# Loading one weight matrix in two transfers of unequal height: 16 partitions, then 112

## The chip, the cores and the metric

The kernel runs on one core of a Trainium2 chip. The metric is the device time of one execution in microseconds, the median of several runs. A core has five instruction streams that matter here: TensorE (PE, with its weight loads shown apart as PEld), VectorE (DVE), ScalarE (ACT), GpSimd (POOL) and SyncE (SP). SyncE computes nothing; it issues the transfers between the chip's main memory (HBM) and the on-chip memory (SBUF, 128 partitions), and those are carried out by 16 DMA engines.

## What is computed

One decode step of a transformer block whose attention and feed-forward halves work side by side on the same normalised input, for 4 sequences and one new token each:

```python
xn = layernorm(x)                                   # x: 4 x 1 x 512
q  = (xn @ wq)                                      # wq: 512 x 4096, 32 heads of 128
p  = softmax(q . k_cache * 128**-0.5)               # k_cache: 4 x 32 x 8192 x 128
o  = (p . v_cache) @ wo                             # v_cache like k_cache; wo: 4096 x 512
f  = (silu(xn @ w_gate) * (xn @ w_up)) @ w_down     # 512 x 1792, 1792 x 512
out = x + o + f
```

All arrays are bfloat16. The two caches are 268 MB each, so nearly all of the bytes that have to be read are keys and values; each is used once.

## The kernel before

SBUF holds three large buffers, `slot[0]` to `slot[2]`, each of 128 partitions by 64 KB. A key tile or a value tile is 8 MB, fills one slot, and covers four heads of one sequence; there are 32 of each. The slots are used in turn: while one tile is being worked on, the next two are on their way. All loads are issued by SyncE, in the order in which the code states them, and a load into a slot waits until the work that reads the slot's old content is done.

A tile of keys is turned in place by VectorE (`turn_k`, line 261), multiplied with the queries by TensorE (`score`, line 268), and the softmax weights of it follow (`max_1`, `max_2`, `pt_turn`). The tile of values that belongs to it is then multiplied with these weights (`pv`, line 310) and the result is scaled (`fin`). `begin` and `finish` hold these pieces; a hardware loop (line 408) walks over the 32 tiles.

The change touches what comes ahead of that loop. `wq_t` is `slot[2]`. The matrix wq (4 MB) goes into the first 32 KB of each partition of that slot, one row of 32 KB per partition, by a single transfer of 128 partitions (line 101). The input x (4 rows) goes into the same slot beside it, by two small transfers (lines 102 and 103). The first key tile goes to `slot[0]` (`load_k(0, 0)`, line 95). These four transfers are issued at once, with nothing to wait for.

When x has landed, VectorE normalises it (lines 156 to 172), TensorE turns it (line 177) and multiplies it with wq (lines 183 to 187), and VectorE and ScalarE bring the queries into their place, `qtn` (lines 193 to 200). `build_q` (line 255) spreads the queries of one tile into `zq`, which the scores need. The three feed-forward matrices are loaded into `slot[2]` as soon as wq has been read (`load_ffn`, lines 219 to 221), then comes the second key tile into `slot[1]`. The first key tile is turned and scored, its slot takes the first values (line 98), and the feed-forward half is computed. Then the loop starts.

After the loop's last round the matrix wo is loaded into a slot in 11 pieces (lines 381 and 385), multiplied piece by piece with the attention output (`wo_mm`), and the sum is stored (lines 449 to 451).

Of the kernel before, what the change touches and what calls it, by code (L numbers as in the profile page):

```python
# [15 lines left out]
def kernel(  # L16
# [13 lines left out]
    nc = tc.nc  # L30
    P = nc.NUM_PARTITIONS

    B, Sq, D = A_x.shape
    _, H, Sk, Dh = A_k_cache.shape
# [3 lines left out]
    EC = D // P  # L38
# [43 lines left out]
    wq_t = slot[2]  # L82
    free = [EC * H * Dh]

    def beside_wq(parts, w, dtype=dt.bfloat16):

        n = w * (2 if dtype == dt.float32 else 1)
        c0 = free[0]
        free[0] += n
        assert free[0] <= SLOT  # L90
        ap = wq_t[0:parts, c0:c0 + n]
        return ap.bitcast(dt.float32) if dtype == dt.float32 else ap
# [4 lines left out]
    def load_v(n, s):  # L97
        nc.sync.dma_start(out=slot[s][:], in_=v_all[bass.ds(n, 1), :, :].rearrange("o p f -> (o p) f"))

    x_sb = beside_wq(B, D)  # L100
    nc.sync.dma_start(out=wq_t[:, 0:EC * H * Dh], in_=A_wq.rearrange("(p c) n -> p (c n)", c=EC))
    nc.sync.dma_start(out=x_sb[0:B - 1, :], in_=x_flat[0:B - 1, :])
    nc.sync.dma_start(out=x_sb[B - 1:B, :].rearrange("b (k e) -> b k e", k=2),
                      in_=x_flat[B - 1:B, :].rearrange("b (k e) -> b k e", k=2))
# [86 lines left out]
    for half in range(NH):  # L191
        for r in range(2):
            nc.vector.transpose(out=qt[:, half, :, r, :],
                                in_=q_ps[half][:].rearrange("p (x i r) -> p x i r", x=8, r=2)[:, :, :, r])
# [285 lines left out]
```

## Time and profile before

| | |
|---|---|
| time, median of 3 runs | 1279.57 us (1279.52 to 1279.66) |
| span of the profiled run | 1278.0 us |
| bytes moved by DMA | 550.90 MB |
| TensorE busy | 694.6 us, 54% |
| VectorE busy | 790.5 us, 62% |
| mean clock granted to TensorE | 0.778 of full speed |

A reader should know four views. The page gives the busy time of each engine, and the span in 40 slices with the share of time that the DMA engines were busy. Its list of DMA issues gives, for each load, how many there were, how large, and the median time from issue to landing; a load that stands in a queue behind others shows a long time there although its own bytes take less. The timeline shows instructions in order of time, with the idle time before each and what ended it. The chain of waits follows the work that ended last back to what released it, step by step.

### The profile page before, as it was taken

To read this page: it belongs to the slowest core of one execution; us is meant where nothing else is said; L and a number is where in the kernel's file an instruction comes from. 1 tells how busy PE (TensorE), PEld (TensorE's weight loads), DVE (VectorE), ACT (ScalarE), POOL (GpSimd) and SP (SyncE) were. 2 spreads that over 40 slices of the span, in tenths; PEclk is the share of its full clock that TensorE was granted. 3 is DMA by queue.
4 is the path that set the end of the run, shared out by engine and by line. 5 is a ranking of instruction groups with operands and counts; after the bars stand their busy time and mean duration, and the time that the engine had idled before them with its cause. 6 is when DMAs were issued, how large, how long until landed. Compare 5 with 4: busy or idle time off the path is not lost.

```text
span 1278.0 us, 11913 instructions
## 1 busy us (share of the span) xinstructions
PE 694.6 (54%) x4507; PEld 306.5 (24%) x4507; DVE 790.5 (62%) x743; ACT 28.8 (2%) x70; POOL 13.1 (1%) x12
## 2 busy tenths in 40 slices
PE   1765455665445665445664446664446654456655
PEld 0322122222212222122222212221222222122222
DVE  5777655666655766655757555766556666556662
ACT  1000000000000000000000000000000000000000
POOL 3000000000000000000000000000000000000000
PEclk9977668877778877678877778876778777688868
DMA  9999999999999999999999999999999999999998
GB/s 401 446 435 429 432 434 441 427 437 431 443 429 429 439 435 437 427 439 433 441 427 437 431 441 431 429 437 437 437 427 439 433 441 427 437 431 441 431 424 346
DMA packets 11689, 550.90 MB, mean 431 GB/s; under 512 B 1304, under 2 KB 1824, under 8 KB 2720
## 3 DMA queue, kind: packets, MB, share of 16 engines
q1 hardware_dynamic: 11680, 550.78, 99.6%
q8 instruction: 6, 0.10, 0.0%
q14 instruction: 3, 0.02, 0.0%
HBM read 550.77 MB, written 0.00 MB: 431 GB/s over the span
## 4 chain that ended last, share of the span: by engine, by line
PE 49%; DVE 22%; another core or an unknown queue 14%; DMA 9%; issue 5%; DVEq 0%; SPq 0%; ACT 0%; PEld 0%; PEldq 0%
PE sps L73 36%; DVE slot L261 12%; PE oacc L73 9%; DMA slot<-in_A_k_cache_dram 7%; DVE ptz L291 4%; DVE zq L255 2%; PE xps L73 2%; DVE oacc L323 2%; DVE o L324 2%; PE mps L73 1%; DMA slot<-in_A_wo_dram 1%; DMA slot<-in_A_x_dram 1%; PE mps L277 1%; DVE rcp L300 0%
## 5 line engine op out<-in xcount | busy, mean ns | idle before, releaser
L73 PE MATMUL sps<-slot,zq 128*128 128x512 bf16 x2048 | 518.2, 417 | 392.2 <-DVE slot L261 392.2
L261 DVE STREAM_TRANSPOSE slot<-slot 128x2048 uint32<-128x2048 uint32 (+1 forms) x194 | 561.5, 2958 | 207.5 <-DMA slot<-in_A_k_cache_dram 207.4
L73 PEld LDWEIGHTS <-zq 128*128 128x128 bf16 x2048 | 211.4, 104 | 686.8 <-issue 343.5
L291 DVE STREAM_TRANSPOSE ptz<-p__117 32x512 bf16<-32x512 bf16 x128 | 89.9, 703 | 86.9 <-PE mps L73 83.9
L73 PE MATMUL oacc<-slot,ptz 128*16 128x512 bf16 x2112 | 130.8, 390 | 7.0 <-issue 3.9
L73 PE MATMUL xps<-rowy,o 128*128 128x4 f32 x66 | 18.3, 348 | 157.6 <-DVE o L324 157.6
L272 DVE TENSOR_REDUCE mx<-sps 128x1 f32<-128x512 f32 x32 | 22.1, 692 | 100.9 <-PE L73 69.3
L73 PEld LDWEIGHTS <-ptz 128*16 128x16 bf16 x2112 | 58.7, 111 | 64.8 <-issue 24.7
L73 PEld LDWEIGHTS xps<-rowy,o 128*128 128x128 f32 x66 | 16.0, 302 | 160.0 <-issue 110.3
L285 ACT ACTIVATE p__117<-sps,nb 128x512 bf16<-128x512 f32 x32 | 22.0, 687 | 1169.9 <-PE oacc L73 758.9
L255 DVE COPY zq<-qtn 32x4 bf16 (+1 forms) x128 | 29.9, 233 | 3.5
L323 DVE TENSOR_TENSOR oacc<-oacc,rowu 128x512 f32<-128x512 f32 x33 | 23.1, 699 | 7.7 <-PE L73 6.7
L324 DVE TENSOR_REDUCE o<-oacc 128x128 f32<-128x512 f32 x33 | 22.8, 691 | 1.1
L280 DVE TENSOR_REDUCE nm<-mps 128x4 f32<-128x64 f32 x32 | 7.2, 224 | 23.4 <-PE L73 23.4
L319 DVE TENSOR_TENSOR otn_nat<-xps,rcp 128x4 f32 (+1 forms) x33 | 5.3, 162 | 23.6 <-PE xps L73 22.2
L73 PEld LDWEIGHTS mps<-rowb,rs 128*128 128x128 f32 x64 | 9.5, 186 | 13.2 <-issue 13.2
L73 PE MATMUL mps<-rowb,rs 128*128 128x4 f32 x64 | 12.3, 263 | 0.0
L277 PE MATMUL mps<-ident_f,mx 128*128 128x128 f32 x32 | 10.5, 328 | 0.0
L373 POOL MEMSET slot<- 128x11264 bf16 x1 | 9.5, 9484 | 18.9 <-DVE qtn L200 18.9
L277 PEld LDWEIGHTS mps<-ident_f,mx 128*128 128x128 f32 x32 | 4.3, 134 | 13.6 <-DVE mx L272 12.4
L73 PE MATMUL yo_ps<-slot,ident 4*4 4x256 bf16 x2 | 0.4, 368 | 13.2 <-DMA slot<-in_A_x_dram 13.2
L300 DVE RECIPROCAL rcp<-mps 128x4 f32<-128x4 f32 x32 | 5.8, 182 | 1.0
(60 smaller groups left out, 64.6 us busy)
## 6 DMA issues: line engine op xcount, KB each, us to landing
slot<-in_A_wq_dram SPq DMA_DIRECT2D x1, 4096.0 KB, 12.3
slot<-in_A_v_cache_dram SPq DMA_DIRECT2D x1, 4096.0 KB, 44.5
slot<-in_A_v_cache_dram SPq DMA_DIRECT2D x2, 2048.0 KB, 50.6
slot<-in_A_wo_dram SPq DMA_DIRECT2D x7, 512.0 KB, 18.2
slot<-in_B_w_gate_dram SPq DMA_DIRECT2D x1, 1792.0 KB, 16.6
slot<-in_B_w_up_dram SPq DMA_DIRECT2D x1, 1792.0 KB, 19.6
slot<-in_B_w_down_dram SPq DMA_DIRECT2D x1, 1792.0 KB, 22.5
slot<-in_A_k_cache_dram SPq DMA_DIRECT2D x32, 51.5
```

The lines of the kernel that those rows point to most:

```text
L73: nc.tensor.matmul(out_ap, lhsT=lhsT, rhs=rhs, start=start, stop=True, skip_group_check=True, **kw)
L255: nc.vector.tensor_copy(out=zq[q0:q1, :, XO + a * QB], in_=qtn[q0:q1, bass.ds(n * 4, 4)])
L261: nc.vector.transpose(out=ap, in_=ap)
L272: nc.vector.reduce_max(out=mx[:], in_=sps[:], axis=AX.X)
L277: nc.tensor.matmul(mps[:, 0:P], lhsT=mx[:, 0:1].to_broadcast([P, P]), rhs=ident_f[:, :], is_transpose=True, start=True, stop=True, skip_gr ...
L280: nc.vector.tensor_reduce(out=nm[:], in_=by_row(mps[:, 0:P]), axis=AX.X, op=ALU.max, negate=True)
L285: nc.scalar.activation(out=p_[:], in_=sps[:], func=ACT.Exp, bias=nb[:, 0:1], scale=qscale, accum_out=rs[:])
L291: nc.vector.transpose(out=ptz[y * QB:(y + 1) * QB, :, y, :, :].rearrange("p s u x -> p s (u x)"), in_=p_[y * QB:(y + 1) * QB, :].rearrange ...
L300: nc.vector.reciprocal(out=rcp[c % NSLOT][:], in_=mps[:, P:P + HT])
L323: nc.vector.tensor_tensor(out=o_, in0=o_, in1=rowu[:].unsqueeze(2).to_broadcast([P, NV, Dh]), op=ALU.mult)
L324: nc.vector.reduce_sum(out=o1[:], in_=o_.rearrange("p u d -> p d u"), axis=AX.X)
L373: nc.gpsimd.memset(slot[2][:, w3:SLOT], 0.0)
```

## The change

The single load of wq becomes two loads from the same source rows into the same place: partitions 0 to 15 first, partitions 16 to 127 after it. Both are issued by SyncE ahead of x and of the first key tile, as the single one was. Such a split lets a small first part be described and started by itself, and it gives each part its own completion. No other line changes; the rest of the program has the same instructions in the same order on every engine.

```diff
     x_sb = beside_wq(B, D)
-    nc.sync.dma_start(out=wq_t[:, 0:EC * H * Dh], in_=A_wq.rearrange("(p c) n -> p (c n)", c=EC))
+    wq_src = A_wq.rearrange("(p c) n -> p (c n)", c=EC)
+    for p0, p1 in ((0, 16), (16, P)):
+        nc.sync.dma_start(out=wq_t[p0:p1, 0:EC * H * Dh], in_=wq_src[p0:p1, :])
     nc.sync.dma_start(out=x_sb[0:B - 1, :], in_=x_flat[0:B - 1, :])
```

## The prediction

> **What bounds the kernel now.** I read the views in this order: the page's rows by slice, its DMA queues, its list of DMA issues, then the windows at both ends of the span, the timeline of the first 35 us, and the chain of waits over the last 20 us. The first three say whether transfers or engines set the pace:
>
> ```profile
> span 1278.0 us, 11913 instructions
> PE 694.6 (54%) x4507; PEld 306.5 (24%) x4507; DVE 790.5 (62%) x743; ACT 28.8 (2%) x70; POOL 13.1 (1%) x12
> DMA  9999999999999999999999999999999999999998
> DMA packets 11689, 550.90 MB, mean 431 GB/s; under 512 B 1304, under 2 KB 1824, under 8 KB 2720
> q1 hardware_dynamic: 11680, 550.78, 99.6%
> slot<-in_A_wq_dram SPq DMA_DIRECT2D x1, 4096.0 KB, 12.3
> slot<-in_A_k_cache_dram SPq DMA_DIRECT2D x32, 51.5
> ```
>
> No compute engine is busy for more than 62% of the span. The one queue that carries the loads keeps its 16 DMA engines busy for 99.6% of it. What is not busy is 0.4% of 1278 us, or 5.1 us, and the ends of the span account for it:
>
> ```profile
> 0.00:1.00 1.00, 0.00 (x0) 0.00 (x0) 0.10 (x2) 0.26 (x1) 0.41 (x5) 1.00 0.00 0
> 5.00:10.00 5.00, 0.00 (x0) 0.00 (x0) 0.00 (x0) 0.00 (x0) 0.00 (x0) 1.00 1.05 452
> 1260.00:1272.00 12.00, 6.15 (x93) 3.38 (x85) 1.55 (x3) 0.00 (x0) 0.00 (x0) 1.00 1.00 407
> 1274.00:1278.00 4.00, 0.45 (x4) 0.09 (x1) 0.41 (x1) 0.36 (x1) 0.00 (x0) 0.50 0.00 1
> ```
>
> The last two columns are the DMA share and GB/s. The share is 0 in the first microsecond and in the last four, and about 1 elsewhere (a packet's bytes are booked at one instant, so short windows swing around 431). Nothing between the ends is idle, so whatever the 16 engines lose in the first 12 us they cannot make up later. The end of the chain of waits says the same; what is waited for last is a transfer:
>
> ```profile
> 1256.72 0.35 PE xps L73 x15
> 1257.08 2.05 PE oacc L73 x13
> 1259.13 13.53 DMA slot<-in_A_wo_dram
> 1272.65 0.04 issue
> 1272.69 1.82 PE yo_ps L73 x16
> ```
>
> And the timeline of the start shows what stands around the load of wq:
>
> ```profile
> 0.75 0.39 SPq L101 DMA_DIRECT2D slot<-in_A_wq_dram  x1
> 1.85 0.36 SPq L95 DMA_DIRECT2D slot<-in_A_k_cache_dram  x1
> 13.21 0.41 DVE L156 CAST slot<-slot 4x512 f32<-4x512 bf16 x1 [8.66 <-DMA slot<-in_A_x_dram]
> 20.08 0.35 SPq L219 DMA_DIRECT2D slot<-in_B_w_gate_dram  x1
> 22.84 0.31 DVE L200 CAST qtn<-slot 128x64 bf16<-128x64 f32 x1
> 24.19 9.07 DVE L255 COPY zq<-qtn 32x4 bf16<-32x4 bf16 x4
> 33.29 17.66 DVE L261 STREAM_TRANSPOSE slot<-slot 128x2048 uint32<-128x2048 uint32 x8
> ```
>
> Four things are to be seen. x lands at 13.2 us only because it queues behind wq. The first key tile is issued at 1.85 us, so its packets stand directly behind. The projection's result is ready at 23.2 us, yet the first turn of keys starts at 33.29 us, so the queries have about 10 us of room. The load of w_gate is issued at 20.08 us, some 13 us before the first keys are in, so the DMA queue does not run dry there.
>
> [...] the issue list holds 81 loads of 128 partitions (1 wq, 32 k, 34 v, 3 FFN, 11 wo); 81 x 16 = 1296, and 3 + 1 + 4 for the two x loads and the store make the 1304 packets under 512 B. [...]
>
> **The change, part by part.** *One more issue on SyncE.* It costs 0.39 us plus a gap of 0.05 us, so 0.44 us. Behind it in SyncE's queue stand the two x loads and the first key load; their packets come after wq's in any case, and wq needs 4.19 MB / 431 GB/s = 9.73 us, which hides the 0.44 us. Cost 0. *One more wait.* The projection's matmuls and the w_gate load into the same buffer now wait for two landings instead of one. Both transfers stand in the same queues in the same order, so it is the later one that counts; nothing is added beyond its landing. *Bytes and packets.* Rows stay 32 KB long, and every engine still gets 1 + 7 = 8 of them. One packet takes 32768 B / (431/16 GB/s) = 1.216 us. By this alone nothing changes.
>
> *The 16 partitions.* [...] The lower end is +2.8: issue to landing of wq is 12.3 us, of which 9.73 is data, so 2.6 us is start and receipt, and I let up to 0.8 us of the waiting overlap with the start. I take 3.65.
>
> *The 112 partitions.* I assume seven consecutive partitions per engine, 16 + 7e to 22 + 7e. [...] The last engine counts[...]: 3 x 1.216 = +3.65 us. [...]
>
> *Sum.* 3.65 + 3.65 = 7.3 us (6.1 to 8.5), all on the path that sets the end, because the queue has no gap later. The work behind it keeps its distances: x lands near 20.5 us, the queries are ready near 30.5, the first keys near 40.6, and w_gate is issued near 27.4, still 13 us before the queue would empty. 1279.57 + 7.3 = 1286.9 us.
>
> **The rivals.**
> *B, only the first transfer pays:* the 112 partitions are dealt so that engines keep out of each other's way. [...] +2.8 to 3.65 us, about 1283.0.
> *C, rows dealt round-robin:* row after row to engine after engine[...]: 8 x 3.65 = +29.2 us, 1308.8. [...]
> *D, [...]* [...] Then only the hidden issue is left, at most 0.44 us: 1279.6 to 1280.0. [...]
> *E, faster:* a small first transfer gets data moving earlier. The whole start and receipt of wq is 2.6 us[...]; a gain of 1 us would be generous: 1278.6, and over 0.2% (2.6 us) would need all of it.
> A wait that takes the place of DMA is not among them: VectorE waits 207 us in all for keys, 30 times, so compute has room in nearly every tile.
>
> **How the numbers follow.** The first case 0.53, B 0.20, C 0.10, D 0.12, E beyond 0.2% 0.03, and 0.02 for a loss of other size. Slower by over 0.2%: 0.53 + 0.20 + 0.10 + 0.02 = 0.85; within 0.2%: D, 0.12; faster 0.03. The likeliest gives 1286.9. The range takes the first case and B (0.73) and, at its low end, most of D (0.12): 1279.8. Its high end, 1290.0, is 1288.1 with the room[...]. C stays outside.
>
> **What would show it.** Packets under 512 B should be 1320 and the queue's packets 11696. The landing of wq's second part should be near 20 us instead of 13.0, the cast of x near 20.5, the DMA share between 1 and 6 us should show few finished bytes[...], and the GB/s in the loop and the 5.4 us from the last wo landing to the end should stay as they were. If the cast of x stays at 13.2 us, D is right[...]; if it comes at 17, B; near 42, C. If the start is late but the span is not longer, the claim that the queue has no later gap is wrong.

## The result, and the profile after

The changed kernel took 1288.34 us (median of 6 runs, 1288.13 to 1288.48) against 1279.58 us before (6 runs, 1279.52 to 1279.68): a ratio of 1.0068, 95% interval 1.0055 to 1.0081, or 8.76 us more. The page and the list of DMA issues after the change, and last, for comparison, the GB/s row of before:

```profile
span 1286.6 us, 11915 instructions
PE 695.2 (54%) x4507; PEld 307.2 (24%) x4507; DVE 789.0 (61%) x743; ACT 28.9 (2%) x70; POOL 13.1 (1%) x12
DMA  9999999999999999999999999999999999999998
GB/s 294 432 427 445 425 435 438 428 438 438 428 436 440 428 436 438 430 436 438 430 434 436 434 432 434 436 432 434 438 426 438 438 428 438 438 428 436 438 422 349
DMA packets 11705, 550.90 MB, mean 428 GB/s; under 512 B 1320, under 2 KB 1840, under 8 KB 2736
q1 hardware_dynamic: 11696, 550.78, 99.6%
slot<-in_A_wq_dram SPq DMA_DIRECT2D x1, 3584.0 KB, 21.2
slot<-in_A_wq_dram SPq DMA_DIRECT2D x1, 512.0 KB, 7.0
GB/s 401 446 435 429 432 434 441 427 437 431 443 429 429 439 435 437 427 439 433 441 427 437 431 441 431 429 437 437 437 427 439 433 441 427 437 431 441 431 424 346
```

The bytes are the same, the engines' busy times differ by at most 1.5 us, and there are 16 packets more, all of them small: 1320 under 512 B, as forecast for a second transfer on 16 engines. The DMA share is still 9 in nearly every slice and the queue still 99.6% busy. This is the point to learn from: the share says that an engine has a packet in hand, not how fast its bytes move. Only the first number of the GB/s row has changed much, from 401 to 294. The windows show where in that first slice (the last two columns are the DMA share and GB/s):

```profile
1.00:5.00 4.00, 0.00 (x0) 0.00 (x0) 1.52 (x6) 1.03 (x1) 3.21 (x6) 1.00 0.92 131
5.00:10.00 5.00, 0.00 (x0) 0.00 (x0) 0.00 (x0) 0.00 (x0) 0.00 (x0) 1.00 1.02 210
10.00:15.00 5.00, 0.00 (x0) 0.00 (x0) 0.00 (x0) 0.00 (x0) 0.00 (x0) 1.00 1.11 315
15.00:20.00 5.00, 0.00 (x0) 0.00 (x0) 0.00 (x0) 0.00 (x0) 0.00 (x0) 1.00 0.86 210
20.00:25.00 5.00, 0.37 (x2) 0.11 (x2) 2.89 (x6) 0.00 (x0) 0.00 (x0) 1.00 1.09 420
```

While wq is loaded, DMA engines that show a share of 0.86 to 1.11 move 131 to 315 GB/s, where the window from 5 to 10 us had 452 before. From the first keys on (20 us), the rate is the old one. The timeline shows that everything behind is later by one and the same amount:

```profile
21.94 0.42 DVE L158 CAST slot<-slot 4x512 f32<-4x512 bf16 x1 [18.95 <-DMA slot<-in_A_x_dram]
28.81 0.35 SPq L221 DMA_DIRECT2D slot<-in_B_w_gate_dram  x1
31.57 0.31 DVE L202 CAST qtn<-slot 128x64 bf16<-128x64 f32 x1
42.03 17.66 DVE L263 STREAM_TRANSPOSE slot<-slot 128x2048 uint32<-128x2048 uint32 x8
```

The cast of x, the load of w_gate, the queries and the first turn of keys were at 13.21, 20.08, 22.84 and 33.29 us; each is 8.73 or 8.74 us later. The chain of waits ends as before with wo, then TensorE and the copy out:

```profile
1276.45 6.28 DMA slot<-in_A_wo_dram
1282.77 0.34 PE yo_ps L73 x2
1283.14 0.36 ACT res L452
```

Before, the chain ended with

```profile
1274.54 0.36 ACT res L450
```

so 8.60 us of the 8.7 lost in the first 21 us are still there at the end.

The trace also has every DMA packet, here and below that of the one profiled execution of each kernel. The sixteen engines work nearly in step: sorted by start, the large packets of the queue fall into steps of 16, which start within 0.67 to 0.93 us of each other before and within 0.43 to 1.26 us after. The table has the median duration of a step's packets in us; the first eight steps carry wq in 32 KB packets, the ninth is the first 64 KB packet of the keys:

```
step                  1     2     3     4     5     6     7     8     9(k)
before              1.98  1.21  1.21  1.21  1.21  1.21  1.21  1.21  2.42
after               3.68  2.76  2.25  1.78  1.67  1.95  2.21  2.09  3.04
```

The first step after the change carries the 16 partitions; of the seven that carry the 112, the fourth and the fifth in the table are the quickest (1.78 and 1.67 us) and none comes down to the 1.21 us of before. Over the nine steps the medians add up to 8.56 us more than before, nearly the whole loss of 8.76 us.

### The profile page after: what moved, and what is told of

The parts are those of the page before. It is cut to its first block, busy times and chain, and to the rows that moved or that the text cites. A ratio compares the mean times of both kernels' runs of the same rounds, so it can differ in the third digit from the quotient of the medians.

```text
span 1286.6 us, 11915 instructions
## 1 busy us (share of the span) xinstructions
PE 695.2 (54%) x4507; PEld 307.2 (24%) x4507; DVE 789.0 (61%) x743; ACT 28.9 (2%) x70; POOL 13.1 (1%) x12
## 2 busy tenths in 40 slices
DMA packets 11705, 550.90 MB, mean 428 GB/s; under 512 B 1320, under 2 KB 1840, under 8 KB 2736
## 3 DMA queue, kind: packets, MB, share of 16 engines
q1 hardware_dynamic: 11696, 550.78, 99.6%
## 4 chain that ended last, share of the span: by engine, by line
PE 48%; DVE 22%; another core or an unknown queue 14%; DMA 9%; issue 5%; DVEq 0%; PEld 0%; SPq 0%; ACT 0%; PEldq 0%
PE sps L73 36%; DVE slot L263 12%; PE oacc L73 9%; DMA slot<-in_A_k_cache_dram 7%; DVE ptz L293 4%; DVE zq L257 2%; PE xps L73 2%; DVE oacc L325 2%; DMA slot<-in_A_x_dram 2%; DVE o L326 2%; PE mps L73 1%; PE mps L279 1%; DMA slot<-in_A_wo_dram 0%; DVE rcp L302 0%
```

## The experiments

Theory P is the prediction's: what a row costs depends on which partitions the sixteen engines write at the same time. Which sets of partitions are slow, and by how much, no trace of before shows; the sizes that P gives are my estimates, put to the test here. Its rivals are S (any transfer under 128 partitions is slow), T (a further transfer costs, wherever it goes), U (a more even cut is better), and later H (all sixteen engines are slowed alike, where P lets each lose for itself).

**Same 512 KB, four ways to place them.** In these four runs wq is loaded whole, by its old single transfer, and another copy of its first 16 rows goes ahead of it into the still empty second slot, where nobody reads it. Only the destination differs (each run has one of these four; the line that defines `wq_src`, as in the change, is left out in this and the later diffs that only add lines):

```diff
+    nc.sync.dma_start(out=slot[1][0:16, 0:EC * H * Dh], in_=wq_src[0:16, :])      # 0, 1 ... 15
+    nc.sync.dma_start(out=slot[1][0:61:4, 0:EC * H * Dh], in_=wq_src[0:16, :])    # 0, 4 ... 60
+    nc.sync.dma_start(out=slot[1][32:93:4, 0:EC * H * Dh], in_=wq_src[0:16, :])   # 32, 36 ... 92
+    nc.sync.dma_start(out=slot[1][:, 0:2048],                                     # 128 rows of 4 KB
+                      in_=wq_src[0:16, :].rearrange("p (a n) -> (p a) n", a=8))
```

> wq stays in one transfer; a copy of its first 16 rows (512 KB) is loaded ahead of it into partitions 0 to 15 of the still empty second slot. It moves 512 KB more, 1.2 us by bytes. Theory P ([...]the loss goes to the end undiminished): +1.2 + 3.65 = +4.9 us, 1284.4, or 1283.6 if 0.8 us of it overlaps with the start. Rival S (what costs is being under 128 partitions, however they lie): the same here. Rival T (what costs is one more transfer): 1.2 plus most of the 8.8 us measured, about 1289.

> The same 16 rows as in the run on partitions 0 to 15, into partitions 0, 4, 8 ... 60[...]. Theory P: +1.2 + 1.2 = +2.4 us, 1282.0. Rival S: as partitions 0 to 15, about +4.9. Rival T: about 1289.

> The same 16 rows, into partitions 32, 36 ... 92[...]. Theory P: +1.2 us, 1280.8, no loss beyond the bytes although it is still 16 partitions in a transfer of its own. Rival S: about +4.9. Rival T: about 1289.

> The same 512 KB of wq, as 128 rows of 4 KB into all 128 partitions of the second slot. Theory P and rival S: +1.2 us, 1280.8. Rival T: about 1289.

Measured against 1279.57 us before: 1283.61 in partitions 0, 1 ... 15 (+4.04), 1281.77 in 0, 4 ... 60 (+2.20), 1280.87 in 32, 36 ... 92 (+1.30), 1280.47 as 128 rows (+0.90). The runs of a kernel agree within 0.9 us but for those in 0, 4 ... 60: seven of these eleven lie between 1281.47 and 1281.88 us, three between 1282.65 and 1283.66, and one took 1295.11, which stays unexplained. The lists of DMA issues give size and time to landing of the extra 16 rows. In partitions 0, 1 ... 15, then 0, 4 ... 60, then 32, 36 ... 92:

```profile
slot<-in_A_wq_dram SPq DMA_DIRECT2D x1, 512.0 KB, 6.5
```

```profile
slot<-in_A_wq_dram SPq DMA_DIRECT2D x1, 512.0 KB, 4.7
```

```profile
slot<-in_A_wq_dram SPq DMA_DIRECT2D x1, 512.0 KB, 3.6
```

The source rows, the number of partitions and the number of packets (11721) are the same in these three; only the set of partitions written differs. The 16 rows in 32, 36 ... 92 cost close to their bytes (1.30 against 1.2 us), so S falls, and so does T. (Why 128 rows cost 0.3 us less than their bytes was not followed up.) Between the slowest and the quickest of the three sets lie 2.74 us. The distance between the partitions is not all that counts: steps of four cost 2.20 us from partition 0 and 1.30 us from partition 32. What makes one set slower than another these runs do not show. The 2.74 us are close to the prediction's lower end (2.8), the one with 0.8 us hidden in the start.

**The same sizes, cut by columns.** The edit is shown against the changed kernel:

```diff
-    for p0, p1 in ((0, 16), (16, P)):
-        nc.sync.dma_start(out=wq_t[p0:p1, 0:EC * H * Dh], in_=wq_src[p0:p1, :])
+    for c0, c1 in ((0, 2048), (2048, EC * H * Dh)):
+        nc.sync.dma_start(out=wq_t[:, c0:c1], in_=wq_src[:, c0:c1])
```

> wq in two transfers of the same sizes as in the change (512 KB and 3.5 MB), but cut by columns: both go to all 128 partitions. Theory P[...]: no loss, 1279.6 to 1280.0. Rival T (a second transfer costs): as the change, about 1288.3.

Measured: 1279.56 us against 1279.60. In the timeline the cast of x stays where it was:

```profile
13.15 0.41 DVE L158 CAST slot<-slot 4x512 f32<-4x512 bf16 x1 [8.60 <-DMA slot<-in_A_x_dram]
```

A second transfer, its issue and its wait cost nothing here. Of the two cuts it is the one across partitions that costs.

**Other cuts across partitions.** The first edit stands against the changed kernel; the second takes the place of both lines of its loop:

```diff
-    for p0, p1 in ((0, 16), (16, P)):
+    for p0, p1 in ((0, 64), (64, P)):                    # rows_64_64
+    for p0 in range(0, P, 16):                           # rows_16_x8
+        nc.sync.dma_start(out=wq_t[p0:p0 + 16, 0:EC * H * Dh], in_=wq_src[p0:p0 + 16, :])
```

> wq in two transfers of 64 partitions. [...] Theory P: half rate throughout, 8 x 1.216 = +9.7 us, 1289.3. Rival U (the small transfer of 16 partitions is what hurts, and a balanced cut would be better than the change): below the change, 1280 to 1284.

> wq in eight transfers of 16 partitions. Theory P: [...]+8 x 3.65 = 29.2 us, 1308.8 (1308 if 0.8 us overlaps with the start). Rival B of the prediction (only a transfer's first rows pay): +3.65. Rival T: seven extra transfers times 8.8 us, 61 us or more.

Measured: 1289.85 us (+10.25) for 64 and 64, 1305.59 us (+25.99) for eight times 16. U falls: the even cut is worse than the change. The median packets, steps as above:

```
step            1     2     3     4     5     6     7     8     9(k)
64 + 64       2.02  2.57  2.57  2.57  2.36  2.57  2.57  2.57  2.74
16, 8 times   3.72  4.49  4.49  4.50  4.50  4.50  4.50  4.50  3.38
```

With 64 partitions to a transfer a 32 KB packet takes 2.57 us in most steps, with 16 neighbouring ones 4.50 us, in the single load of 128 it took 1.21 us: 2.1 and 3.7 times as long for the same number of bytes. Worked out from these medians, the sixteen engines together move 204, 116.5 and 433 GB/s. The eight times 16 came out 2.4 to 3.2 us below its expectation; seven packets of 4.50 instead of 4.86 us account for 2.5 of that.

**Is the dealing of the 112 rows as assumed?** Here the one transfer of 112 is spelled out as seven transfers of 16 rows, in place of the single load of wq:

```diff
+    nc.sync.dma_start(out=wq_t[0:16, 0:EC * H * Dh], in_=wq_src[0:16, :])
+    for j in range(7):
+        nc.sync.dma_start(out=wq_t[16 + j:122 + j:7, 0:EC * H * Dh], in_=wq_src[16 + j:122 + j:7, :])
```

> wq as partitions 0 to 15 and then seven transfers of 16 rows, 16 + j, 23 + j ... 121 + j for j = 0 to 6: the order in which I think the one transfer of 112 is carried out, spelled out. If 112 partitions go as seven consecutive rows to each engine, the time is that of the change, 1288.3, and the packets step by step take the same; if they are dealt in another way, another time (round-robin would be the run of 16 eight times, 1305.6).

Measured: 1288.50 us against 1279.63, +8.87. Its steps take 3.63, 2.79, 2.23, 1.77, 1.79, 2.00, 2.19, 2.11 and 3.02 us, the change's within 0.12 us each. In this run the partitions of each step are known, since each transfer of 16 rows is one step: the step at 16, 23 ... 121 is the slowest of the seven (2.79 us), those at 18, 25 ... 123 and 19, 26 ... 124 are the quickest (1.77 and 1.79 us). All this fits seven consecutive rows per engine in the change, and rules out round-robin, which is the run of eight times 16 (1305.59 us).

**Which engines lose?** One step of the 112 by itself, as extra rows ahead of the whole wq:

```diff
+    nc.sync.dma_start(out=slot[1][16:122:7, 0:EC * H * Dh], in_=wq_src[0:16, :])
```

> wq in one transfer; ahead of it the 16 rows into partitions 16, 23, 30 ... 121 of the second slot, which is the first step of the 112 partitions as I deal them[...]. Theory P with each engine losing for itself: [...]the last counts: +1.2 + 1.2 = +2.4 us, 1282.0. Rival H ([...]by what the trace after the change shows[...], about 0.8 us): +2.0 us, 1281.6, and all engines equally late. If the 112 are dealt in another way this run says nothing of it.

Measured: 1281.44 us (+1.84), 0.54 us more than in partitions 32, 36 ... 92. Both theories had forecast more, so the time alone leaves both open; the packets decide. If only some of the engines lost, the others would begin their third packet when the engines of the run in 32, 36 ... 92 did, at 4.93 to 5.35 us. All sixteen began it between 5.63 and 6.15 us. The landings agree. The trace has sixteen of them for such a transfer, one for each row: in 32, 36 ... 92 the extra rows landed at 3.91 to 4.34 us, here at 4.56 to 5.73 us, so that the earliest here is later than the latest there. In this run, then, all sixteen engines were slowed, as H says.

In the changed kernel it is the same: all sixteen engines begin their second key packet at 23.32 to 24.22 us (before: 14.44 to 15.12). The prediction let the last engine lose 3.65 us for itself; had others lost nothing, the engines would be about that far apart. They are 0.90 us apart (before: 0.68). Why they come out alike was not tried.

Three runs repeated such a step four times with 16 KB rows, in three sets of partitions, to tell P from H by the time:

```diff
+    for i in range(4):
+        nc.sync.dma_start(out=slot[1][A:B:S, i * 8192:(i + 1) * 8192],
+                          in_=wq_src[0:16, (i % 2) * 8192:(i % 2 + 1) * 8192])
```

> wq in one transfer; ahead of it four transfers of 16 rows of 16 KB (1 MB in all) into partitions 32, 36 ... 92 of the second slot[...]. Both theories: the bytes alone, 1.05 MB / 431 GB/s = +2.4 us, 1282.0.

> The same four transfers into partitions 18, 25 ... 123[...]. Theory P, each engine loses for itself: [...]1284.7. Theory H, [...]([...]1.67 to 1.78 us for 32 KB after the change): 0.85 us for every engine, +4 x 0.24 = 1.0: 1283.0.

> The same four transfers into partitions 16, 23 ... 121[...]. Theory P: [...]1284.7. Theory H: 1.0 to 1.1 us for every engine ([...]1.95 to 2.21 us for 32 KB), +4 x 0.45 = 1.8: 1283.8[...].

A:B:S is 32:93:4, 18:124:7 and 16:122:7 in turn. Measured against 1279.63: 1284.46, 1284.37 and 1284.10 us. These times tell nothing of the sets: 32:93:4, the quick one before, is 2.4 us above its bytes, as late as the others, and its own runs spread from 1283.41 to 1285.09. Why four small transfers in a row cost twice their bytes stays open.

The landings in the profiled runs limit what H says. At 32:93:4 the sixteen rows of the first transfer land at 3.40 to 3.73 us and those of the second at 4.04 to 4.34. At 16:122:7 eleven rows of the first land at 3.29 to 3.68 us, in time, and five at 4.07 to 4.44; of the second transfer fifteen rows land after 4.34 us, up to 5.58. So at first only five of the sixteen rows were late, and nearly all of them one small row later. At 18:124:7 even the second transfer has fourteen rows in time or nearly so (3.94 to 4.41 us) and two late (4.92 and 5.47): there these runs do not show H. From the third transfer on the run at 32:93:4 is slow as well, fifteen of its packets taking 0.82 to 1.09 us instead of 0.61, so nothing later can be put down to the set of partitions.

## Why the prediction was right, point by point

*The bound.* Right: no gap in the queue takes up a loss at the start; 8.73 us at the cast of x, 8.60 us at the last copy. The work behind did keep its distances, at the end too. The 5.4 us of the prediction were misread: they count from the landing at 1272.65 us, which is that of the seventh of the eleven pieces of wo. The last piece landed at 1274.03 us before and at 1282.73 us after (+8.70), with 4.0 and 3.9 us left to the end.

*The further issue and wait cost nothing.* Right: the cut by columns has both and is at -0.04 us.

*The 16 partitions, +3.65 us.* Right in kind, too high in size: 2.74 us by the runs in 0, 1 ... 15 and in 32, 36 ... 92. The 3.65 us, three packets of 1.216 us, were my estimate; no trace of before showed them. Two things fit the smaller size, and were not told apart: part of the loss may hide in the first packet's own start (1.98 us before, for what takes 1.21 later), as the lower end supposed, and a step of 16 neighbouring partitions takes 4.50 us (eight times 16), which is 3.29 us above the 1.21 us of the single load and not 3.65.

*The 112 partitions, +3.65 us.* The dealing was right; the time was wrong. I let each engine lose for itself and took three packets for the one that loses most, again an estimate that no trace of before showed. In the changed kernel all came out about equally late instead. By difference the part is worth 8.76 - 2.74 = 6.0 us, outside the 2.4 to 4.9 that the range of the sum leaves for it, and paid by all sixteen engines. The medians of steps 2 to 8 agree: together they are 6.24 us longer than before.

*The sum, +7.3 us, 1286.9.* Measured +8.76. The two terms were off by -0.9 and +2.35 us, so they covered for each other in part, and that is luck. The 6.1 to 8.5 given for the sum varies the second term only; with the lower end of the first it would begin at 5.2, and 8.76 lies above its end either way. The range to 1290.0 held because it left room above the first case; what filled that room, the lateness of all engines, it did not foresee.

*The rivals.* B (only the first transfer pays) falls with the 6.0 us; C (round-robin) with the run spelled out by hand; D (only the further issue is left) with the three placements of the same rows; E needed a faster start, and the first packets were slower (3.68 us instead of 1.98). Of the signs named, the packet counts came exactly; the cast of x came at 21.94 us, not near 20.5, and between 1 and 5 us 131 GB/s were moved (287 before), few as forecast.

## What to carry to other kernels

A load that is cut across partitions is not the same load in two pieces: here the pace of the same bytes depended on the partitions that were written, from 1.21 us for 32 KB in the load of 128 to 4.50 us in loads of 16 neighbours. Read it from the durations of the packets, step by step. If a load has to come in pieces, try the cut along the row, with 128 partitions in each piece; that was free here (1279.56 against 1279.60 us). And in a kernel whose DMA queue never runs dry (99.6% busy here), a loss in the first microseconds is a loss at the end (8.73 us at the cast of x, 8.60 us at the last copy), while the DMA share stays at 9 in nearly every slice.

## What the runs showed of the hardware

- A 32 KB packet took 1.21 us in the load of 128 partitions, 2.57 us in most steps of 64 and 64, and 4.50 us in most steps of eight times 16 (medians).
- The same 16 rows, put into partitions 32, 36 ... 92, then 0, 4 ... 60, then 0, 1 ... 15, landed 3.6, 4.7 and 6.5 us after their issue and cost 1.30, 2.20 and 4.04 us of the whole time.
- Two loads of wq cut by columns, 128 partitions each, took 1279.56 us against 1279.60 with the single load.
- Sixteen rows in partitions 16, 23 ... 121 slowed all sixteen engines within one 32 KB row each: landings at 4.56 to 5.73 us instead of 3.91 to 4.34 in 32, 36 ... 92. With rows of 16 KB eleven of the first sixteen rows still landed in time (3.29 to 3.68 us; 3.40 to 3.73 in 32, 36 ... 92).
- Packets ended before their bytes counted as landed: the last packet of the change's first 16 rows ends at 6.05 us and the transfer lands at 7.71; with the single load of wq before the change it was 12.70 and 13.00 us.
- A DMA share of 0.86 to 1.11 went with 131 to 315 GB/s while wq came in two loads (windows from 1 to 20 us; the share from 1 to 5 us was 0.92), and 1.09 with 420 GB/s once the keys followed (20 to 25 us).
